# A three-layer kernel on one core: every step from the first load to the last store in one written list, in a new order

## The chip, the cores and the metric

The kernel runs on one core of one Trainium2 chip. The metric is the device time in microseconds (us) of that core, the median of several executions. One more execution was profiled, and all rows below come from it. Its engines are called PE (TensorE), DVE (VectorE), ACT (ScalarE), POOL (GpSimd) and SP (SyncE, whose queue issues the transfers).

## The reference

Three layers follow one another (float32 throughout):

```python
scores = scale * q @ k.T                    # 4 batches x 8 heads, 576 tokens, 64 wide
masks  = local (last 32 keys) for heads 0-3, strided (same position mod 32) for heads 4-7
attn   = softmax(where(mask, scores, -1e9)); x = (attn @ v) as 2304 x 512

h = relu(x @ w_in) ** 2                     # 512 -> 2048
x = h @ w_out                               # 2048 -> 512

logits = x @ phi                            # 2304 x 32 slots
d = softmax(logits, over the tokens); slot_input = d.T @ x
slot_out[e] = relu(slot_input[e] @ w1[e]) @ w2[e]     # 8 experts, 4 slots each
out = softmax(logits, over the slots) @ slot_out
```

## The kernel before, in words

The tokens go in five blocks of 512, 512, 512, 512 and 256. The hidden width of the second layer is cut into 16 pieces of 128, so that there are 80 **steps** (16 to a block, `NSTEP`). One step is 12 matmuls of 128 by 128 by 512 (by 256 in the last block), issued by `gemm1` in four quarters of three: a product of a high and a low part in a reduced float format. Its result lies in one of two PSUM buffers called `h`. `square` takes it out with a relu (token R), `sq` squares it (X; on ACT, or on POOL for some early steps), `bt_` turns it in 32x32 blocks on DVE (T), and `logits` multiplies four steps at a time with a folded matrix `pt` (L), in four column strips of the array.

At the end of each block `Dispatch` carries a running softmax over the tokens: `copy`, `total` (two full-array matmuls and a maximum), `turn`, `slots` (up to 64 small products in 32x32 tiles of the array, into the PSUM tile `four`), `sums` (adds them to the block sums) and `comb` (the softmax over the slots). The last block has its own path, `last_turn` and `last_sums`, after which the expert layer runs: `slot_in`, `sit`, `gemm_a`, `relu`, `turn`, `gemm_b`, `slot_out` and `output`. While the last step's softmax runs, `hold` issues five dummy matmuls.

Beside this run 16 attention units (`Unit`, token A: four masks and score products per batch, a softmax on DVE, ACT and POOL, turned weights, value products) and 24 conversions (`convert`, token C), which unpack weights that lie in memory as 64-bit words. Their PE work uses the array in strips of 32 or 64 columns, except masks and subtractions.

**What sets the order.** Each engine has its own queue and takes its instructions in the order in which the program issues them; only semaphores tie the queues together. Up to step 17 the order is a written list of tokens, `HEAD`, each a letter, a number and sometimes an engine (`A0P` is the next step of unit 0, on POOL). From step 18 on, a loop issues the four quarters of each step in turn, and after each quarter what a table of positions says (`AT`, `OFF`, `WO_AT`, `D_AT`, `LATE_T` and others):

```python
for kc in range(4):
    if s >= HEAD_STEPS:
        gemm1(s, (0, 2, 1, 3)[kc:kc + 1])
    if kc == 3 and s >= HEAD_STEPS:
        (last_step if s == NSTEP - 1 else square)(s)
    for fn, args in bg.get(4 * s + kc, ()):
        fn(*args)
```

The expert layer is plain straight code after the loop. The 64 weight tiles of the experts (512 KB each) are loaded in one fixed order `e_order` by `load_e`, each into a buffer that something else has left; SP issues them in program order and waits there for the buffer.

Of the kernel before, what the change touches and what calls it, by code (L numbers as in the profile page):

```python
# [29 lines left out]
OLD_AT = (8, 6)  # L30
# [3 lines left out]
WO_AT = [91, 117, 154, 170, 199, 219, 235, 249]  # L34
AT = [76, 89, 101, 115, 131, 150, 163]
OFF = [0, 7, 8, 12, 23]
# [3 lines left out]
w9 A0 A0 A0D A0P A0 A0 A0P A0A A2P q2 A2P A2 A0D w6 l2 C1 l3 C1 C1 A2P A2D A2 A2 A0P A0A A0A A0A A0A A0A A0A C1D q1  # L40
A1D A1P A1A A1 l1 v0 A0A A0A A2D C1 C1P C1P C1D A1A A1D A1 A2 A2D A2D A1 l0 C0 C0 A2A A2A A2A A2A A2A A2A C0 A1D C1P
C0 A3 A0A q3 A3 A3 A0 A0A A1A A3D C0 C0A C0P C0P A0A A0 A1A A1A A1D A3D A1A A3D v2 A2A A2D A3A A1A A1A A1A A1A G0 l5
l4 C2P C2P A3P A3P A2D A2D A2D A2 C0P A2 A3A A2 A2A v1 A1D G0 G1 A3A A3A A3A C2 A1 A1A A1P C2P C2 C2P A1 l6 q4 A4D A4
G1 C3D A3A A3A A3A A3A l7 C3 A4D A4D A4 v3 H A3A A3 C3 A3 C3P A3 C3 A3 C3 C3P C3P C2 A3 A3 A3 A3 G0 G1 G1 A4A R1 G0 R0
A5A C3D C2D A4D A4D l9 l10 C5D l11 C5 C5 C5 C5 l8 C4D C4 C4 C4P C4 C4D C4P C5 C5P C5D C5P G3 G3 G3 G3 R3 C2D G4 G4 G4
G4 q5 l17 A4 A5A A5 A5 l16 C8 C8 l12 C6 R4 C8 C4P C8 l14 l13 C6D C6 C6 G2 G2 A5 A5P A5 A5D A4P C4P G2 G2 C7 l18 A5D
X4A C6 R2 l15 C7 C7P l19 C9 C9D C9 C7 C9 C8 A4A C7D C9P A4A A5A C7P C6 A4A C7P C7P G5 A6 G5 G5 G5 G6 G6 G6 G6 G7 G7 G7
q6 A6A A6 l21 f P0 G7 A6D G9 G9 R5 A4D T4 X3D R6 P0 P0 A4A A4A R7 A5 C6D C6P X1D A4A Z v4 A4 A5P A6P A6P A5 X0A P0 C7P
X2A T1 T2 A4 A4A A5 A5 A4 A4A A4 C6P A4 G9 G9 G10 G10 G8 G8 G8 A5 l23 l20 C10P C10D C10D C10 R9 C10P l24 l22 C11 C11
C11 C11 C11 A4A A4P A6 X7A T7 A6P A6P A6A G10 G10 P1 P1 G8 v5 q7 A7 A7A G11 C12 R8 X6A A7P l25 C12 C12 G11 G11 G11 R10  # L50
C12 C12 X5A R11 A7D A7D A5 G14 A6P A6D l26 X9D A7A A7P A7D A7D A5 A7A A7P A7D A5 A7A A5P C13 l27 C13 C13 A7A A5A C13
C13 A5 G12 G12 G12 G12 R12 X12A T3 A7A A7P G14 G14 G14 R14 T0 G13 G13 P1 P1 P2 L0 P2 P2 P2 T9 l28 C14A q8 v6 A6A l29
C14 X14A A6A A6A A6 C14 X11A X8D A6P A7A A6 A6 G15 G13 G13 R13 C14 l30 C15 A8A L1 A6P A6 v7 A8 A8 C14P A8 A8A X13A
X10A T5 A7P A7A A7 A7 A7A A8P l31 C15 C15 A8 A8 C15 A8D T11 G15 G15 G15 T10 G17 G17 G17 G17 G16 G16 G16 G16 C15D P3
A8P A8D A8 A8 A8 R15 X15D A8 A8 A8 A8 L2 T15 P3 P3 P3 v8 A8 T8 A8 R16 A8D A8 A8 T13 T12 T6 T14 R17 L3
"""
FILL = 6
HEAD_STEPS = 18
AT_LAST = 40
ATT_END = 48  # L60
D0_AT = [1, 9, 11, 14, 17, 19]
D_AT = [3, 6, 7, 12, 13, 17]
DZ_AT = [7, 11, 17, 23, 30, 32]
LATE_T = 16
LATE_L = 22
LG_OFF = 19
LATE_TZ = 26
LATE_LZ = 37
EPS = 1e-9
HOLD = [5, 0, 0]  # L70
# [22 lines left out]
def body(tc, qd, kd, vl, vs, win, wout, woutt, phi, w1, w2, cst, out):  # L93
# [3 lines left out]
    with ExitStack() as base, ExitStack() as order:  # L97
# [464 lines left out]
        class Dispatch:  # L562
            def __init__(self, b):
                self.b, self.T = b, TB[b]
                self.n = TB[b] // 128
                self.cv = c_all[:, 4 * b:4 * b + self.n, :]

# [44 lines left out]
            def sums(self):  # L612
                for n in range(2):
                    to, flat = acc[:, 2 * DM * n:2 * DM * n + 2 * DM], four_[n].rearrange("p a z -> p (a z)")
                    if self.b >= KEEP:
                        return
                    if self.b:
                        DVE.scalar_tensor_tensor(out=flat if self.b == KEEP - 1 else to, in0=to, scalar=al, in1=flat, op0=ALU.mult, op1=ALU.add)
                    else:
                        DVE.tensor_copy(to, flat)  # L620

            def last_turn(self):
                z = [slice(0, 128), slice(128, 256)]
                e_ = gk_[0][:, 0:256]
                for n in range(2):
                    ACT.activation(e_[:, z[n]], self.o[:, z[n]], AF.Exp, bias=nm, accum_out=(bs, bs2)[n])
                    DVE.transpose(out=lsb[:, z[n]], in_=e_[:, z[n]])
                ACT.activation(al, nm_run, AF.Exp, scale=-1.0, bias=nm)
                DVE.tensor_scalar_mul(tal, tident[:, 0:NS], al)
                ov = self.o[:, 0:256].rearrange("p (c a i) -> p c a i", a=4, i=32)  # L630
                for a in range(4):
                    DVE.transpose(out=self.cv[q(a)], in_=ov[q(a), :, a, :])

            def last_sums(self):
                o = [ps("h", f"accT{x}") for x in range(2)]
                old = gk_[0][:, OLD:OLD + 2048].rearrange("p (a z) -> p a z", a=4)
                to = {}
                for x in range(2):
                    for n, copy in enumerate((ACT.copy, DVE.tensor_copy)):
                        z = 2 * x + n  # L640
                        to[x, n] = (lsb if z == 3 else gk_[0][:, 512 * z:512 * z + 512]).rearrange("p (a i) -> p a i", a=2)
                        copy(to[x, n], four_[n][:, :, 256 * x:256 * x + 256])
                for x in range(2):
                    for a in range(4):
                        PE.matmul(o[x][q(a), 0:256], tal, old[:, a, 256 * x:256 * x + 256], start=True, stop=False, skip_group_check=True)
                for x in range(2):
                    hold(HOLD[1 + x])
                    for a in range(4):
                        PE.matmul(o[x][q(a), 0:256], tident[:, 0:NS], to[x, a // 2][:, a % 2], start=False, stop=True, skip_group_check=True)
                    DVE.transpose(out=gT[:, 8 * x:8 * x + 8, :].rearrange("p f s -> p (f s)"), in_=o[x][:, 0:256])  # L650
# [86 lines left out]
        convs = [convert(m) for m in range(16)]  # L737
        mats = [matrix(h) for h in range(4)]
        gemms = {s: iter((0, 2, 1, 3)) for s in range(HEAD_STEPS)}
# [7 lines left out]
        for token in HEAD.split():  # L747
            k, e = token[0], token[-1] if token[-1] in ENG else ""
            n = int(token[1:].rstrip("ADP") or 0)
            if k == "f":  # L750
                SP.dma_start(ph, phi)
            elif k == "q":
                load_qk(units[n].b, units[n].p, units[n].u)
            elif k == "v":
                load_v(units[n].b, units[n].p, units[n].u)
            elif k == "l":
                load_w(n)
            elif k == "w":
                for _ in range(n):
                    PE.matmul(warm, dummy, dummy, start=True, stop=True)  # L760
            elif k == "A":
                units[n].step(e)
            elif k == "C":
                next(convs[n])(e)
            elif k == "P":
                next(mats[n])()
            elif k == "G":
                gemm1(n, (next(gemms[n]),))
            elif k == "R":
                square(n, e)  # L770
            elif k == "X":
                sq(n, e)
            elif k == "T":
                bt_(n)
            elif k == "L":
                logits(0, n)
            elif k == "H":
                headx.close()
                gp.append(pool(base, "gp", reuse_waits="tile"))
                gt_.append(gp[0].tile([128, SB * 512], F32, name="gt"))  # L780
                gk_.append(gp[0].tile([128, NG * 512], F32, name="gk"))
            else:
                psx.close()
                lgp = pool(lgx, "lgp", space=PSUM, reuse_waits="tile")
                four_.extend(lgp.tile([128, 2, 512], F32, name=f"four{n}") for n in range(2))

        bg = {}

        def at(p, fn, *args):
            bg.setdefault(p, []).append((fn, args))  # L790

        end0 = 4 * SB
        last = AT_LAST
        for n, p in zip(range(9, 4 + len(UNITS)), AT):
            un = units[n]
            at(max(end0, last + 3), load_qk, un.b, un.p, un.u)
            at(max(end0, last + OFF[4]), load_v, un.b, un.p, un.u)
            for k, o in zip("SCETV", OFF):
                at(p + o, un.run, k)
            last = p  # L800
        for b in range(NBLK):
            e = end0 * b
            late_t, late_l = (LATE_TZ, LATE_LZ) if b == NBLK - 1 else (LATE_T, LATE_L)
            if b:
                for f in range(SB):
                    p = 4 * (SB * b + f) + 4
                    at(p, sq, SB * b + f)
                    at(max(p, e + late_t), bt_, SB * b + f)
# [43 lines left out]
        for n in range(3):  # L852
            at(WO_AT[0] - 16 + n, load_wo, n)
# [244 lines left out]
```

## Time and profile before

| | us |
|---|---|
| median of 3 executions | 376.4 (376.33 to 376.76) |
| the profiled execution, its own time | 375.84 |
| its span, first to last instruction | 373.8 |
| PE busy in it | 361.2 |
| DVE / ACT / POOL busy | 243.8 / 173.5 / 63.8 |

The span is what the rows divide; 2.04 us of the profiled execution's own time lie around it. Busy time of PE is modelled from pipelined matmuls, so a busy PE can still lose time between two matmuls; the lengths of runs of matmuls in the chain show that better than the busy share.

### The profile page before, as it was taken

What the parts mean: (1) busy time and instruction counts of PE and PEld (TensorE: products, weight loads), DVE (VectorE), ACT (ScalarE), POOL (GpSimd) and SP (SyncE); (2) the same over time, 40 slices, a digit from 0 to 9 for tenths busy, and PEclk for the clock granted to TensorE, in tenths of its full rate; (3) what the DMA queues carried; (4) which work ended last, traced back from release to release, by engine and by line L of the source; (5) the groups of instructions that cost most, each with busy time, mean ns of one, the idle gap of its engine ahead of it and who ended that gap; (6) DMA issues with size and microseconds to landing.
All of it is one profiled execution on the core that took longest, in us unless ns stands there. A gap on an engine that the chain in (4) does not pass through costs nothing.

```text
span 373.8 us, 9705 instructions
## 1 busy us (share of the span) xinstructions
PE 361.2 (97%) x4062; PEld 260.4 (70%) x4062; DVE 243.8 (65%) x516; ACT 173.5 (46%) x373; POOL 63.8 (17%) x96
## 2 busy tenths in 40 slices
PE   8979999999999999999999999999999999999993
PEld 7767876676756687786677877667778698534783
DVE  2798999999997698787598763484243454432251
ACT  1697594555532454453246435425454445211241
POOL 7153339210120012020002100000000000262000
PEclk9999999999999999999999999999999999999999
DMA  8999966566516026334123158240318999999986
GB/s 233 359 350 351 393 212 225 167 211 185 187 45 246 3 67 210 94 121 119 60 63 107 50 196 302 91 183 15 115 56 289 413 408 357 335 400 412 407 346 240
DMA packets 25356, 80.59 MB, mean 216 GB/s; under 512 B 3041, under 2 KB 3297, under 8 KB 25313
## 3 DMA queue, kind: packets, MB, share of 16 engines
q1 hardware_dynamic: 25072, 79.53, 59.7%
q8 instruction: 32, 0.52, 0.6%
q10 hardware_dynamic: 240, 0.44, 0.5%
q14 instruction: 12, 0.09, 0.1%
HBM read 75.25 MB, written 4.72 MB: 214 GB/s over the span
## 4 chain that ended last, share of the span: by engine, by line
PE 80%; DVE 13%; issue 2%; POOL 2%; ACT 2%; DVEq 0%; ACTq 0%; POOLq 0%
PE h L479 47%; PE four L608 6%; PE so L983 4%; PE eh L956 4%; PE oa L396 3%; PE four L532 2%; PE lg L532 2%; DVE y L454 2%; DVE ptl L366 1%; PE out L1001 1%; DVE wo L454 1%; PE ob L396 1%; PE qa L291 1%; DVE w L463 1%; DVE tiny L322 1%
## 5 line engine op out<-in xcount | busy, mean ns | idle before, releaser
L479 PE MATMUL h<-x,w 128*128 128x512 f32 x768 | 188.3, 398 | 0.2 <-ACT gk L498 0.2
L479 PEld LDWEIGHTS h<-x,w 128*128 128x128 f32 x768 | 140.9, 188 | 46.1 <-issue 15.2
L498 ACT ACTIVATE gk<-h 128x512 f32<-128x512 f32 (+1 forms) x70 | 38.4, 551 | 86.5 <-PE h L479 86.2
L511 DVE STREAM_TRANSPOSE gt<-gk 128x512 f32<-128x512 f32 (+1 forms) x71 | 44.3, 640 | 44.7 <-ACT gk L502 39.0
L502 ACT ACTIVATE gk<-gk 128x512 f32<-128x512 f32 (+1 forms) x68 | 39.5, 584 | 1.4
L479 PEld LDWEIGHTS h<-xl,w 128*128 128x128 f32 x192 | 23.6, 191 | 3.5 <-issue 3.4
L479 PE MATMUL h<-xl,w 128*128 128x256 f32 x192 | 25.0, 287 | 0.0
L366 DVE STREAM_TRANSPOSE ptl<-sl 32x320 f32<-32x320 f32 (+1 forms) x48 | 23.7, 493 | 0.7
L447 ACT ACTIVATE wo<-raw 128x512 f32<-128x512 f32 x32 | 20.8, 669 | 5.8 <-DVE w L463 3.7
L454 DVE SCALAR_TENSOR_TENSOR wo<-raw,wo 128x512 uint32<-128x512 uint32 x32 | 22.3, 715 | 0.2
L608 PE MATMUL four<-gt,lsb 32*32 32x512 f32 x576 | 21.3, 598 | 0.0
L608 PEld LDWEIGHTS four<-gt,lsb 32*32 32x32 f32 x576 | 9.7, 103 | 8.5 <-issue 3.8
L412 DVE TENSOR_TENSOR x<-oa,x 128x512 fp32r<-128x512 f32 (+1 forms) x16 | 10.7, 666 | 6.9 <-ACT x L411 4.6
L463 POOL TENSOR_TENSOR w<-y,w 128x512 fp32r<-128x512 f32 x11 | 15.0, 1373 | 0.6 <-ACT w L459 0.5
L817 POOL COPY lsb<-pt 128x128 f32<-128x128 f32 x1 | 0.3, 289 | 84.8 <-PE four L608 84.8
L983 PE MATMUL so<-e,gk 128*32 128x128 f32 (+1 forms) x304 | 14.7, 302 | 0.0
L956 PE MATMUL eh<-e,lsb 128*32 128x512 f32 x104 | 14.3, 594 | 0.4 <-DVE lsb L934 0.4
L366 DVE STREAM_TRANSPOSE pts<-sw 32x512 f32<-32x512 f32 x20 | 14.0, 700 | 0.7 <-POOL sw L331 0.5
L459 POOL CAST w<-y 128x512 fp32r<-128x512 f32 x9 | 8.8, 985 | 30.9 <-DVE y L454 7.6
L411 ACT CAST x<-oa 128x512 fp32r<-128x512 f32 (+1 forms) x15 | 9.0, 601 | 10.8 <-PE oa L396 10.5
L315 POOL TENSOR_TENSOR sl<-sl,tiny 128x640 f32<-128x640 f32 x4 | 5.4, 1340 | 49.4 <-DVE tiny L314 49.4
L450 DVE TENSOR_SCALAR wo<-wo 128x1024 uint32<-128x1024 uint32 x16 | 12.5, 784 | 0.7 <-ACT wo L447 0.5
(231 smaller groups left out, 480.8 us busy)
## 6 DMA issues: line engine op xcount, KB each, us to landing
e<-w SPq DMA_DIRECT2D x50, 512.0 KB, 8.1
raw<-win SPq DMA_DIRECT2D x16, 512.0 KB, 8.2
raw<-woutt SPq DMA_DIRECT2D x16, 512.0 KB, 4.9
raw<-wout SPq DMA_DIRECT2D x16, 512.0 KB, 4.0
q<-qd SPq DMA_DIRECT2D x16, 288.0 KB, 4.4
out<-ob SPq DMA_DIRECT2D x12, 384.0 KB, 4.2
k<-kd SPq DMA_DIRECT2D x29, 144.0 KB, 4.2
v<-vs SPq DMA_DIRECT2D x8, 512.0 KB, 4.9
```

The source lines that it names most:

```text
L366: yield "T", lambda e, d=dst, s_=src: DVE.transpose(out=d, in_=s_)
L396: PE.matmul(o[bank][d0, col:col + w1_ - w0], u.v[0:k, t, d0], rhs, start=start, stop=stop, skip_group_check=True)
L447: ACT.activation(y[0][:, z], raws[2 * m + z][:, :, 1].bitcast(F32), AF.Prelu, scale=2.0 ** -112, alpha=2.0 ** 32)
L454: DVE.scalar_tensor_tensor(out=yb, in0=raws[2 * m + z][:, :, 0], scalar=29, in1=yb, op0=ALU.logical_shift_right, op1=ALU.bitwise_or)
L463: ENG[e].tensor_tensor(out=w[:, 1], in0=y[0][:, z], in1=w[:, 0].bitcast(F32), op=ALU.subtract)
L479: PE.matmul(hs[s][0][:, 0:TB[b]], w_in[s % SB][:, a, 128 * kc:128 * kc + 128], x_of(b, kc)[:, x, :] if b < 4 else xl[:, :, kc, x, :], star ...
L498: ACT.activation(gs[s], h[:, 0:TB[s // SB]], AF.Relu)
L502: ACT.activation(gs[s], gs[s], AF.Square)
L511: DVE.transpose(out=by_tokens(b)[:, :, f, :] if b else gt_[0].rearrange("p (f t) -> p f t", f=SB)[:, f], in_=gs[s])
L608: PE.matmul(four_[a // 2][q(c % 4), a % 2, :], ext[q(a), c, :], g[q(a), c] if self.b else g[q(a), :, 32 * c:32 * c + 32], start=c < 4 and ...
L956: PE.matmul(hps[g][n][q(j), :], siT[:, kc, :], cols(et[0, g, j, kc], 512 * n, 512), start=kc == 0, stop=kc == 3, skip_group_check=True)
L983: PE.matmul(sums[n][q(j)], hT[g][fc // 4][:, fc % 4, q(j)], cols(et[1 + n, g, j, wd * fc // 1024], wd * fc % 1024, wd), start=g == 0 and f ...
```

## The change

`HEAD` now holds all tokens from the first load to the last store, with new letters for the later work (D for the parts of `Dispatch`, K for one dummy matmul, E `gemm_a`, z a part of `gemm_b`, F one output product and its copy, d one output store, and lower-case letters for expert loads). The loop, its tables and the straight code go. The functions keep what they compute; `last_turn`, `last_sums`, `turn`, `output` and others are cut into pieces so that each piece can stand anywhere. PE gets the same matmuls as before, five dummies among them. What differs, besides the order:

- the first block's sums are copied by ACT (one half) and DVE, before by DVE alone;
- 21 of the 79 relus of `square` are on DVE, before none;
- 31 of 79 squares are on POOL, before 5 (a token `X..D` takes the POOL branch of `sq`);
- 21 of the copies of attention values out of PSUM are on DVE, before 5;
- in the last six output products DVE copies the first, third and fifth result, before ACT did;
- the steps of the second layer are no longer in rising order.

```diff
-OLD_AT = (8, 6)
-WO_AT = [91, 117, 154, 170, 199, 219, 235, 249]
-AT = [76, 89, 101, 115, 131, 150, 163]
-OFF = [0, 7, 8, 12, 23]
...
-HEAD_STEPS = 18
...
-D_AT = [3, 6, 7, 12, 13, 17]
...
-HOLD = [5, 0, 0]
...
 HEAD = """
...
+q2 w9 A2P A0 A0 A0D A0P A0 A0 A0P A0A A0P A2P w6 A1D l2 C1 l3 C1 A2 A2P A2D C1 A0P A0A A0A A0A A2 A0A C1D C1 A0A A0A
+q1 A1P A1A C1P C1P A2 A2P A1 C1D A0A A0A A1A A1D A1 A3 l0 C0 l1 C0 A2 A2D A2A A1 A2A A2A v0 A0A A2A A2A A2A A2A C0 A0
...
+D0 T8 D0 G20 G20 G20 G20 G19 G19 G19 G19 T14 R18 T13 R20D l32 q9 v9 A9P D0 A9P T17 T16 R19 A9P A9P A9P X18A C16 A9P
...
+G59 G59 G63 G63 G63 C23 C23 C23 C23 R59 X62D G60 G60 G60 G60 R60D G63 T57 X59A X58D L14 X60A T60 G64 G64 G64 R63 X63D
...
+G68 G68 G71 G71 G71 G71 G69 G69 G69 G69 G70 D3 D3 R68 R71 R69 x1 x2 i0 c0 c1 i1 s0 r0 r1 r2 s1 s2 s3 s4 G70 G70 G70
...
+X64A T64 D3 G77 G77 R77D G75 G75 G75 G75 R75 T65 D3 X73D X75D X77A T67 G76 G76 G76 G76 G78 G78 G78 G78 G79 R76 X76D m0
+T70 L16 L17 L18 T71 T73 T77 T75 T74 R78 X78A T76 T72 o1 T78 L19 D4 o0 G79 G79 G79 R79 T79 K0 D4 u3 T66 a0 K0 K0 K0 K0
+a1 V0 D4 b1 b3 B0 b0 N0 b2 Q0 B1 N1 u0 s5 g0 s6 s7 s8 s9 s10 s11 I0 I1 I2 s12 s13 s14 s15 i2 g1 s16 s17 s18 s19 x3 x4
+I3 x5 x6 p0 S0 E1 E0 E2 W0 M3 u1 p1 S1 E3 k0 k1 k2 k3 c0 E4 E5 c1 r0 r1 r2 E9 E8 E10 E6 E12 E7 k4 k5 s0 s1 s2 u2 D4 U0
...
+z5 z5 z5 z5 z5 z5 z5 F16 F17 d8 F15A F14D d7 z5 z5 z5 z5 z5 z5 z5 z5 t2 F18D F19A d9 F20D F21A d10 F22D F23A d11
 """
...
-                        DVE.tensor_copy(to, flat)
-
-            def last_turn(self):
...
+                        (DVE.tensor_copy if n else ACT.copy)(to, flat)
+
+            def last_exp(self, n):
                 e_ = gk_[0][:, 0:256]
...
+            def last_scale(self):
                 ACT.activation(al, nm_run, AF.Exp, scale=-1.0, bias=nm)
                 DVE.tensor_scalar_mul(tal, tident[:, 0:NS], al)
...
+            def last_copy(self, z):
+                x, n = divmod(z, 2)
+                t = self.to[x, n] = (lsb if z == 3 else gk_[0][:, 512 * z:512 * z + 512]).rearrange("p (a i) -> p a i", a=2)
+                (DVE.tensor_copy if n else ACT.copy)(t, four_[n][:, :, 256 * x:256 * x + 256])
...
+        def hold(n):
+            PE.matmul(late_ps("at", "hold0")[:, 0:256], ident, c[:, 0:256], start=True, stop=True)
...
+        def product(x, e):
+            d, n, z = x // 6, x // 2 % 3, x % 2
+            o = late_ps(("h", "at", "h", "at", "t")[x % 5], f"out{d}{n}{z}")
+            PE.matmul(o[:, 0:TO], tiles["s4"][:, 1, 128 * d:128 * d + 128],
+                      cT[n][:, 3 * z:3 * z + 3, :].rearrange("p a b -> p (a b)"), start=True, stop=True)
+            (DVE.tensor_copy if (e or "AD"[x % 2]) == "D" else ACT.copy)(ob(d, n)[:, z], o[:, 0:TO])
...
+        for token in HEAD.split():
...
+            elif k == "R" and n == NSTEP - 1:
+                last_step(n)
+            elif k == "R":
+                square(n, e)
...
+            elif k == "D":
+                next(disps[n])()
```

## Rows read from the trace of the kernel before

**Rows 1.** The page: busy time and share of the span of each engine, and instructions.
```profile
PE 361.2 (97%) x4062; PEld 260.4 (70%) x4062; DVE 243.8 (65%) x516; ACT 173.5 (46%) x373; POOL 63.8 (17%) x96
```

**Rows 2.** Stretches: length, busy PE, PEld, DVE, ACT, POOL (instructions), granted clock, DMA share, GB/s.
```profile
0.00:30.00 30.00, 25.52 (x382) 21.11 (x383) 19.52 (x50) 17.70 (x43) 13.74 (x28) 1.00 0.97 320
30.00:120.00 90.00, 88.48 (x934) 63.34 (x948) 83.81 (x161) 50.81 (x107) 26.93 (x23) 1.00 0.65 222
120.00:160.00 40.00, 40.00 (x460) 29.29 (x435) 31.83 (x67) 17.79 (x35) 5.95 (x6) 1.00 0.30 94
```

**Rows 3.** Waits of TensorE: who was waited for, us, times, longest.
```profile
PE wide L271 <- DVE tiny L265: 1.3, 2, 0.7
```

**Rows 4.** The chain that ended last, 240 to 300 us: start, length, what.
```profile
252.15 9.07 PE h L479 x39
261.22 1.00 PE lg L532 x8
262.21 11.11 PE h L479 x48
...
288.21 0.86 PE lr L576 x2
```

**Rows 5.** Groups by line and shape, VectorE: busy, mean ns, idle before.
```profile
L463 DVE TENSOR_TENSOR w<-y,w 128x512 fp32r<-128x512 f32 x5 | 4.6, 950 | 0.0
...
L620 DVE COPY acc<-four 128x1024 f32<-128x1024 f32 x2 | 2.3, 1194 | 0.0
...
L459 DVE CAST w<-y 128x512 fp32r<-128x512 f32 x2 | 1.6, 808 | 0.0
...
L642 DVE COPY gk<-four 128x512 f32<-128x512 f32 x1 | 0.7, 691 | 1.8 <-PE four L608 1.8
...
L411 DVE CAST x<-oa 128x256 fp32r<-128x256 f32 x1 | 0.6, 610 | 0.0
...
L411 DVE CAST xl<-ob 128x64 fp32r<-128x64 f32 x1 | 0.2, 224 | 0.0
```

**Rows 6.** Line 504, the squares on GpSimd: ns least/median/most, first and last start.
```profile
L504 POOL TENSOR_TENSOR gk<-gk x2: 1042/1266/1490, 74.2 to 103.6; 128x512 f32<-128x512 f32 x2
```

**Rows 7.** Line 450 on VectorE, same columns.
```profile
L450 DVE TENSOR_SCALAR wo<-wo x16: 650/684/1657, 47.3 to 279.2; 128x1024 uint32<-128x1024 uint32 x16
```

**Rows 8.** Order of time, 45 to 52 us: start, length, engine, line.
```profile
45.52 4.55 POOL L463 TENSOR_TENSOR w<-y,w 128x512 fp32r<-128x512 f32 x3
...
47.26 1.66 DVE L450 TENSOR_SCALAR wo<-wo 128x1024 uint32<-128x1024 uint32 x1 [0.49 <-ACT wo L447]
```

**Rows 9.** Order of time, 312 to 332 us.
```profile
317.03 0.67 PE L578 MATMUL lr<-gk,lsb 128*128 128x256 f32 x2 [0.27 <-ACT gk L520]
...
317.54 2.32 PE L895 MATMUL hold<-c 128*128 128x256 f32 x10
...
319.79 2.38 PE L608 MATMUL four<-gt,lsb 32*32 32x512 f32 x64
...
328.63 1.92 PE L956 MATMUL eh<-e,lsb 128*32 128x512 f32 x16 [0.37 <-DVE lsb L934]
```

**Rows 10.** Order of time, the last 20 us.
```profile
363.23 3.29 PE L983 MATMUL so<-e,gk 128*32 128x128 f32 x64
...
367.74 1.24 ACT L1003 COPY ob<-out 128x384 f32<-128x384 f32 x3 [0.91 <-PE out L1001]
367.91 1.49 DVE L1003 COPY ob<-out 128x384 f32<-128x384 f32 x3 [0.71 <-PE out L1001]
```

**Rows 11.** SyncE queue: loads of the last layer, first two and last groups.
```profile
220.20 9.20 SPq L683 DMA_DIRECT2D e<-w  x7
...
247.69 0.86 SPq L683 DMA_DIRECT2D acc<-w  x2
...
340.90 9.26 SPq L683 DMA_DIRECT2D e<-w  x8
```

**Rows 12.** The page, transfers: issues, KB each, median us from issue to landing.
```profile
e<-w SPq DMA_DIRECT2D x50, 512.0 KB, 8.1
```

More of the change, by code (lines that the diff above doesn't have):

```diff
@@ L787, in body @@
[L787 to L808, printed above, removed]
-                for ch in range(4 if b < NBLK - 1 else 3):
-                    at(max(e + 16 * ch + LG_OFF, e + late_l), logits, b, ch)
-            if b < NBLK - 1:
-                d = Dispatch(b)
-                for o, f in zip(D0_AT if b == 0 else DZ_AT if b == NBLK - 2 else D_AT, (d.copy, d.total, d.turn, d.slots, d.sums, d.comb)):
-                    at(e + end0 + o, f)
@@ L824, in body, with tile_of, late_ps, bt @@
-        cs4, cT, co = {}, {}, {}
-        def weights(n, eng):
+        gT = pt
+        siT = lsb[:, 0:128].rearrange("p (a b) -> p a b", a=4)
+        rsum = st[:, 14:15]
+        tiles = {}
+        def tile_of(name, make):
+            if name not in tiles:
+                tiles[name] = make()
+            return tiles[name]
+        def late_ps(tag, name):
+            return tile_of(name, lambda: ps(tag, name))
+        def bt(n):
+            return gk_[0][:, 512 * n:512 * n + 512]
+        def hT(g, n):
+            return bt(2 + 2 * g + n).rearrange("p (a b) -> p a b", a=4)
@@ new lines, in relu, with turn @@
+        def relu(x):
+            g, n = divmod(x, 2)
+            if n:
+                DVE.tensor_scalar(bt(1), hps(g, 1), rsum, 0.0, op0=ALU.mult, op1=ALU.max)
+            else:
+                ACT.activation(bt(0), hps(g, 0), AF.Relu, scale=rsum)
+        def turn(x):
+            g, n = divmod(x, 2)
+            ht = late_ps("mo" if n else "t", f"ht{g}{n}")
+            for z in range(4):
+                h_ = bt(n)[:, 256 * (z // 2):256 * (z // 2) + 256].rearrange("p (x a) -> p a x", a=2)[:, z % 2, :]
+                PE.matmul(ht[:, 128 * z:128 * z + 128], h_, ident, start=True, stop=True, is_transpose=True)
@@ L846, in weights_t, with weights_out @@
                           is_transpose=True)
[L848 removed]
+        def weights_out(x, e):
+            n, z = divmod(x, 2)
             cT[n] = cs4[n]
[L850 to L860 removed]
@@ L862, in body, with sums @@
-        for s in range(SB, NSTEP + 1):
-            if s == ATT_END:
+            (DVE.tensor_copy if (e or "DA"[z]) == "D" else ACT.copy)(cT[n][:, 3 * z:3 * z + 3, :].rearrange("p a b -> p (a b)"),
+                                                                      tiles[f"ct{n}{z}"][:, 0:384])
+        cuts = [slice(0, 256), slice(256, 384), slice(384, 512)]
+        def sums(n):
+            o = late_ps(("t", "lg", "t")[n], ("so0", "so1", "so0")[n])
+            return o[:, (0, 0, 256)[n]:(256, 128, 384)[n]]
@@ new lines, in output, with load_e_one, final @@
+        def output(x):
+            d, n = divmod(x, 3)
+            t0 = 2 * TO * n
+            SP.dma_start(out[128 * d:128 * d + 128, t0:t0 + 2 * TO], ob(d, n).rearrange("p a b -> p (a b)"))
+        def load_e_one(x):
+            load_e(lambda name: ring(x // 4, x % 4, [128, 2, 512], F32, name))
+        def final(n):
+            lgx.close()
+            late.append(pool(base, "late", space=PSUM, reuse_waits="tile"))
+        parts = [parts_b(n, g) for n in range(3) for g in range(2)]
+        plain = {"K": hold, "u": lambda n: d.last_turn(n), "a": lambda n: d.last_exp(n), "V": lambda n: d.last_scale(),
+                 "b": lambda n: d.last_copy(n), "B": lambda n: d.last_old(n), "N": lambda n: d.last_new(n), "Q": final,
+                 "I": slot_in, "p": si_copy, "S": sit, "M": lambda n: POOL.memset(bt(2 + n), 0.0), "E": gemm_a, "U": inverse,
+                 "W": weights, "J": relu, "h": turn, "O": weights_t, "z": lambda n: next(parts[n]), "t": slot_out, "d": output,
+                 "k": load_e_one}
```

444 lines of the change are left out of this document (166 added, 278 removed).

## The prediction

> **What bounds the kernel now.** I read the page's busy times first, then the stretches, TensorE's waits, the chain that ended last, and the order of time where the chain leaves TensorE. The page says that TensorE is busy 361.2 of 373.8 us [rows 1], so at most 12.6 us are idle. The stretches show where: 4.48 us lie in the first 30 us, and from 30 to 160 us TensorE lacks only 1.52 us [rows 2]. TensorE's list of waits is short: its longest total is 1.3 us, for a maximum in the first units [rows 3]. So neither idle time nor waits hold much, and the matmuls themselves do not change.
>
> What is left is time that TensorE loses while it counts as busy. The chain gives it. A run of 39 matmuls of the second layer takes 9.07 us and one of 48 takes 11.11 us [rows 4]. The nine more cost 2.04 us, 0.2267 us each. But 48 times that is 10.88 us, so each run pays 0.23 us once for having been interrupted. The interruption between them is a product with the folded matrix in four column strips: 8 records, two passes for each of 4 strips side by side, 1.00 us [rows 4]. Two such passes over 512 columns on the whole array, the `total` of a block, take 0.86 us [rows 4]. So the strips lose another 0.14 us, and one **visit** from the full array to strips or small tiles and back costs 0.14 + 0.23 = 0.37 us without any idle time.
>
> The second resource is VectorE. From 30 to 120 us it is busy 83.81 of 90 us, from 120 to 160 us 31.83 of 40 [rows 2], so it nearly ties with TensorE there. It has 6.19 + 8.17 = 14.36 us to spare until 160 us.
>
> **The change part by part.**
>
> *Fewer visits.* I wrote both orders down as TensorE's queue sees them and counted the visits (a `total` or a dummy uses the full array and makes none). Until 64 quarter steps have been issued, both orders make 16. After that the order of before makes 29 until the last step, the new one 16: attention products, `slots` and L products now stand side by side, as L16, L17 and L18 do. 13 visits by 0.37 us are 4.8 us. Inside a merged visit the array may still go from strips to 32x32 tiles; such inner changes rise from 6 to 11 in all. No row prices one by itself: five more cost between nothing and half a visit each, 5 by 0.185 = 0.9 us. I take half, 0.5, since strips to tiles is the same kind of change in small: **-4.3 us** (-4.8 to -3.9).
>
> *The end of the last block.* One dummy now stands before `total`. Before, TensorE idled 0.27 us there for the last square, with a further gap inside the busy time, and the five dummies (10 records, 2.32 us) ended at 319.86, where `slots` began at 319.79 [rows 9]. With four after the maximum, `slots` may come up to 0.4 us earlier: -0.4. The first product of the expert layer waited 0.37 us for a VectorE turn [rows 9]; now the second copy stands behind that turn: -0.2. Against this, VectorE has seven turns, a copy of 1024 columns and another turn (about 5 us by the order) just before the last step's square, in some 4.5 us of TensorE work: +0.2 (nothing to +0.5). The output products stood in four groups and stand in five, one visit more: +0.3. At the very end VectorE's three copies take 1.49 us and ScalarE's 1.24, and VectorE began 0.17 us later [rows 10]; starting it first saves that: -0.2. Together **-0.3 us** (-1 to +0.6).
>
> *The head.* The two masks that were issued late are now issued ahead of products, into the holes of the first 30 us. 15 dummies, the loads and their order stay. Of 4.48 idle us [rows 2] and the 1.3 us wait [rows 3], I take **-0.5 us**; the bounds are -2 (half of the idle time closes) and +1.5 (a mask in front of something that was ready).
>
> *Work moved to VectorE and GpSimd.* Up to step 27 the new order puts 8 relus on VectorE. No row has a relu there; the nearest is its copy of 128x512 out of PSUM, 0.691 us [rows 5]: 5.5 us. 7 more copies of attention values come, some of 0.61, some of 0.22 us [rows 5]: 2.8 us. Two weight subtractions more (0.95 each) and two casts fewer (0.81 each) give +0.3, and half of the first block's sums goes, 1.19 us [rows 5]. That is 7.4 us more on VectorE in the stretch where 14.36 are free. The free time is partly waiting that new work cannot fill, so I let a part show: **+0.7 us** (nothing to +7.4). ScalarE has room for its half of the sums: it idles more than half of the span [rows 1]. If that cover went, it would cost one copy of 1024 columns, 1.19 us by VectorE's row.
>
> *GpSimd's squares.* 31 squares go there, before 5. One takes between 1.04 and 1.49 us [rows 6]. Each is off TensorE's path as long as the turn behind it isn't due. What they can do to VectorE the trace shows once: while GpSimd ran three subtractions on end from 45.52 on, VectorE's shift at 47.26 took 1.66 us [rows 8], where the median of that line is 0.684 [rows 7]. So an overlap can cost VectorE 1.0 us. Up to step 27 the new order has 8 squares on GpSimd where 5 were, three more, so at most +3 us where VectorE is tight; the other 23 fall later, and after 160 us VectorE has 243.8 - 135.2 = 108.6 us of work in 213.8 [rows 1, 2]. I take nothing for it in the sum and keep +3 for the range. The Trainium skill (GPSIMD Engine Reference, Specifications) says that GpSimd's SBUF interfaces are shared with VectorE and contend with instructions with two SBUF inputs or in a two-port mode; the shift row agrees with it. By that rule, at the row's price, the three squares would make the sum below 3.0 us larger, 375.0 for a median; without it the sum stands as it is.
>
> *Order of the expert loads.* Only the first stands early in the list (x0), eight others that were issued at 220 and 247 us [rows 11] stand behind step 69. But SP's queue runs ahead of the others: between x0 and those eight there is nothing else on it, so they start when x0 does and their buffers are free. That is after the last conversion of weights, in the new order near step 57, some 260 us. The fixed order of the tiles stays. I count nothing.
>
> **Sum.** -4.3 - 0.3 - 0.5 + 0.7 = -4.4 us against the profiled execution's own 375.84: 371.4. The median of the runs shown is 376.4, 0.56 above that execution, so for a median I forecast 371.4 + 0.6 = **372.0 us**.
>
> **The rivals.**
>
> *The head closes too.* Half of the 4.48 idle us and the whole visit price: 376.4 - 4.8 - 0.3 - 2.2 = **369.1**. For it: only that stretch has idle time on TensorE. Against it: 15 dummies and the first loads stay.
>
> *VectorE becomes the bound, slower.* It gets 7.4 us by step 27 and up to 3 from GpSimd, 10.4 in all, and of its 14.36 idle us it can fill only a share. The other terms give -5.1. With half of it filled, 10.4 - 7.2 = 3.2, and the kernel still gains; with a quarter, 10.4 - 3.6 = 6.8 and it ends 1.7 us slower, **378.1**. It decides from where less than 10.4 - 5.1 = 5.3 of the 14.36 us are of use. For it: 83.81 of 90 us busy. Against it: turns and subtractions may lie behind TensorE for some microseconds, since their results are due only at the end of a block.
>
> *The changes of shape stay.* If a merged visit pays inside what it saves outside (an L product behind `slots` drains the array all the same), the first term is near nothing and head, end and VectorE cancel: **376.3**. Against it: inner changes rise by only 5, and the two passes of `total` show that the price belongs to the shape.
>
> *Loads late, slower.* If the nine early tiles only start after 280 us, nine of 512 KB at the spacing of the last group (9.26 us for 8 [rows 11]), 10.4 us, come onto a queue that is full until 350 us. The last eight tiles, issued until 350.16 [rows 11], land 8.1 us later [rows 12], at 358.3, and the last 64 products, which use half of them, start at 363.23 [rows 10], so 5.0 us of delay are free: 376.4 - 4.4 + 5.4 = **377.4**. It needs the last conversions to be late by 20 us.
>
> **How the numbers follow.** Forecast 0.60 (its own range 370 to 374.6), head closes 0.17, shapes stay 0.08, VectorE 0.11, loads 0.04. The range 368.3 to 376.6 holds the forecast, most of the head case and the shapes case, some 0.83; it leaves out the two slower cases. 0.2% of 376.4 is 0.75 us, about what a measurement of this kernel can tell from no change. Faster by more: 0.60 + 0.17 and a little of the rest, 0.78. Within: 0.08. Slower: 0.11 + 0.04, less what ends even, 0.14.
>
> **What would show it.** In the profile of the changed kernel: TensorE's busy time about 4 us lower, its runs of second-layer matmuls longer and fewer, 0.2267 us each as before. From 30 to 160 us VectorE busy some 7 us more, TensorE still without idle time there. `slots` of the last block right behind the fourth dummy. It is wrong if TensorE's waits name a VectorE relu or a turn, if idle time appears between 100 and 170 us, if VectorE's two-input instructions lengthen in the stretches with GpSimd's squares, or if weight loads in the last 40 us wait for a transfer.

## The result, and the profile after

The changed kernel takes 373.24 us in the median of 4 runs (372.71 to 373.84), the kernel before 376.49 (4 runs, 376.33 to 376.76). The ratio is 0.9913, with a 95% interval of 0.9896 to 0.9931: 3.25 us faster, where 4.4 were forecast. The profiled execution took 373.05 us, its span 371.2.

The page's busy times and the stretches, with the columns of [rows 1] and [rows 2]:

```profile
PE 357.3 (96%) x4062; PEld 262.1 (71%) x4062; DVE 260.0 (70%) x557; ACT 144.0 (39%) x308; POOL 82.6 (22%) x120
...
0.00:30.00 30.00, 24.48 (x383) 20.05 (x384) 19.09 (x50) 17.28 (x40) 16.99 (x31) 1.00 0.97 312
30.00:120.00 90.00, 88.58 (x883) 64.72 (x897) 83.44 (x165) 47.93 (x100) 23.93 (x22) 1.00 0.63 212
120.00:160.00 40.00, 39.40 (x575) 29.22 (x544) 34.18 (x74) 13.63 (x26) 8.46 (x9) 1.00 0.38 117
```

TensorE is busy 3.9 us less, as foreseen. But against [rows 2] it has 0.60 us of idle time from 120 to 160 us, which the prediction had named as a sign that it was wrong, and VectorE is busy only 2.0 us more from 30 to 160 us (83.44 + 34.18 against 83.81 + 31.83), not 7.

The price of an interruption is unchanged. This is the chain that ended last around 270 us, start, us, what (compare [rows 4]):

```profile
267.76 0.99 PE lg L548 x8
268.76 11.11 PE h L495 x48
279.87 0.99 PE lg L548 x8
280.87 3.82 PE h L495 x30
```

What is new stands in the merged visits. The chain again, at 144 and at 224 us, each from the end of one run of second-layer matmuls to the start of the next:

```profile
144.00 0.69 PE qa L324 x53
144.68 0.88 PE four L548 x7
145.56 0.35 issue
145.91 1.24 PE oa L412 x32
147.16 0.18 PE ob L412 x16
147.34 2.76 PE h L495 x11
...
224.52 0.99 PE four L548 x8
225.52 0.50 PE oa L412 x32
226.02 0.50 PE ob L412 x32
226.52 1.83 PE four L548 x8
228.35 2.97 PE h L495 x12
```

At 145.56 TensorE stands for 0.35 us. The value products read attention weights that VectorE turns (L382), and the last of these turns ends at 145.82; the first weight load of the products starts at 145.88. In VectorE's queue the turns stand behind subtractions for the values of the unit before (L428). The timelines (columns: start, us, engine, line, operation, operands, idle time before):

```profile
144.63 0.22 DVE L428 TENSOR_TENSOR xl<-ob,xl 128x32 fp32r<-128x32 f32 x1
144.86 0.96 DVE L382 STREAM_TRANSPOSE ptl<-sl 32x320 f32<-32x320 f32 x2
145.88 1.00 PEld L412 LDWEIGHTS oa<-ptl,v 128*32 128x32 f32 x32 [1.23 <-issue]
```

A third merged visit, at 155.7 us, has 0.25 us of idle time at 157.84, for another reason. There the value products need a PSUM buffer that the scores just before still hold, and the reading of the scores (L314), which ends at 157.99, stands behind a relu that now lies on VectorE (L512). The two waits make the 0.60 us of idle time above:

```profile
156.51 0.69 DVE L512 TENSOR_SCALAR gk<-h 128x512 f32<-128x512 f32 x1
157.23 0.76 DVE L314 SCALAR_TENSOR_TENSOR sl<-qa,c 128x128 f32<-128x128 f32 x2
158.06 0.56 PEld L412 LDWEIGHTS oa<-pts,v 128*32 128x32 f32 x32 [1.13 <-issue]
```

The visit at 224 us shows no idle matmul at all, but its second L product takes 1.83 us where one alone takes 0.99. The weight loads and GpSimd's timeline give the reason:

```profile
227.30 0.14 PEld L548 LDWEIGHTS four<-gk,pt 128*32 128x32 f32 x2 [0.84 <-POOL gk L520]
...
226.21 1.04 POOL L520 TENSOR_TENSOR gk<-gk 128x512 f32<-128x512 f32 x1 [6.13 <-ACT gk L514]
```

The product waits 0.84 us for the square of step 47, which GpSimd ends only at 227.25.

The end of the last block, TensorE's timeline (before: [rows 9, 10]):

```profile
314.18 0.67 PE L595 MATMUL lr<-gk,lsb 128*128 128x256 f32 x2
314.68 1.89 PE L786 MATMUL hold<-c 128*128 128x256 f32 x8
316.53 2.37 PE L625 MATMUL four<-gt,lsb 32*32 32x512 f32 x64
...
325.44 1.07 PE L821 MATMUL eh<-e,lsb 128*32 128x512 f32 x8 [0.37 <-DVE lsb L807]
...
364.76 1.53 PE L906 MATMUL out<-c,s 128*128 128x384 f32 x6 [0.75 <-DVE s L897]
```

By milestones, after less before: first matmul of step 18 109.56 against 110.69, -1.1 us, with the same matmuls behind it; last `total` 314.18 against 317.03, -2.85; `slots` 316.53 against 319.79, -3.26; first expert product -3.19; last output products 364.76 against 367.26, -2.50; end of the span -2.6. So in this pair of executions **the head gave 1.1 us, the middle 1.7, and the end of the last block with the expert layer gave back 0.25**.

The middle, from step 18 to the last `total`, can be added up from TensorE's rows. The second layer has 744 matmuls there in both kernels: before they stand in 33 runs of 156.25 us together, after in 20 runs of 153.65 us, so 13 fewer runs save 2.6 us. The 28 visits before take 47.18 us, and the 15 of the changed kernel, 13 fewer, take 47.91: the visits themselves gave nothing.

One execution is not the kernel. In e7 and e12 below, whose lists are the same in the middle, it takes 203.98 and 203.96 us, in this execution 204.62 and before 206.34. So the middle gained 1.7 us in this execution and 2.4 us in those two. The difference lies in one visit, shown under e3.

### The profile page after: what moved, and what is told of

The parts are those of the page before. It is cut to its first block, busy times and chain, and to the rows that moved or that the text cites. A ratio compares the mean times of both kernels' runs of the same rounds, so it can differ in the third digit from the quotient of the medians.

```text
span 371.2 us, 9694 instructions
## 1 busy us (share of the span) xinstructions
PE 357.3 (96%) x4062; PEld 262.1 (71%) x4062; DVE 260.0 (70%) x557; ACT 144.0 (39%) x308; POOL 82.6 (22%) x120
## 3 DMA queue, kind: packets, MB, share of 16 engines
HBM read 75.25 MB, written 4.72 MB: 215 GB/s over the span
## 4 chain that ended last, share of the span: by engine, by line
PE 71%; DMA 12%; DVE 10%; POOL 2%; ACT 2%; issue 1%; SPq 0%; POOLq 0%; ACTq 0%
PE h L495 41%; PE four L625 6%; DMA raw<-win 5%; PE so L889 4%; PE eh L821 4%; DMA raw<-woutt 3%; PE four L548 2%; PE oa L412 2%; DVE ptl L382 2%; DMA k<-kd 2%; PE lg L548 2%; DMA v<-vs 2%; PE out L906 1%; DVE wo L470 1%; DMA q<-qd 1%
## 5 line engine op out<-in xcount | busy, mean ns | idle before, releaser
L495 PE MATMUL h<-x,w 128*128 128x512 f32 x768 | 184.9, 397 | 0.0
L514 ACT ACTIVATE gk<-h 128x512 f32<-128x512 f32 (+1 forms) x51 | 28.3, 555 | 81.3 <-PE h L495 63.6
L520 POOL TENSOR_TENSOR gk<-gk 128x512 f32<-128x512 f32 (+1 forms) x29 | 27.4, 954 | 103.4 <-ACT gk L514 83.8
L527 DVE STREAM_TRANSPOSE gt<-gk 128x512 f32<-128x512 f32 (+1 forms) x71 | 42.9, 629 | 9.7 <-PE four L625 6.0
L518 ACT ACTIVATE gk<-gk 128x512 f32<-128x512 f32 (+1 forms) x41 | 23.5, 591 | 8.4 <-DVE gk L512 8.1
L382 DVE STREAM_TRANSPOSE ptl<-sl 32x320 f32<-32x320 f32 (+1 forms) x48 | 23.7, 494 | 3.7 <-POOL sl L347 2.9
L512 DVE TENSOR_SCALAR gk<-h 128x512 f32<-128x512 f32 (+1 forms) x19 | 11.6, 610 | 18.1 <-PE h L495 16.2
L466 DVE TENSOR_SCALAR wo<-wo 128x1024 uint32<-128x1024 uint32 x16 | 11.0, 686 | 10.9 <-ACT wo L463 10.6
L382 DVE STREAM_TRANSPOSE pts<-sw 32x512 f32<-32x512 f32 x20 | 14.0, 702 | 1.4 <-POOL sw L347 1.1
L475 POOL CAST w<-y 128x512 fp32r<-128x512 f32 x10 | 7.4, 746 | 28.8 <-ACT gt L514 11.7
L889 PEld LDWEIGHTS so<-e,gk 128*32 128x32 f32 x304 | 11.5, 110 | 3.2 <-issue 1.3
L548 PE MATMUL four<-gk,pt 128*32 128x512 f32 x78 | 11.9, 596 | 0.0
```

The lines of the kernel that those rows point to most:

```text
L382: yield "T", lambda e, d=dst, s_=src: DVE.transpose(out=d, in_=s_)
L495: PE.matmul(hs[s][0][:, 0:TB[b]], w_in[s % SB][:, a, 128 * kc:128 * kc + 128], x_of(b, kc)[:, x, :] if b < 4 else xl[:, :, kc, x, :], star ...
L514: ACT.activation(gs[s], h[:, 0:TB[s // SB]], AF.Relu)
L518: ACT.activation(gs[s], gs[s], AF.Square)
L520: POOL.tensor_tensor(out=gs[s], in0=gs[s], in1=gs[s], op=ALU.mult)
L527: DVE.transpose(out=by_tokens(b)[:, :, f, :] if b else gt_[0].rearrange("p (f t) -> p f t", f=SB)[:, f], in_=gs[s])
```

## The experiments

All medians are of repeated runs beside the kernel before on the same chip. It took 376.3 us (17 runs) beside e1 to e4, 376.63 (14 runs) beside e5 to e8 and 376.66 (13 runs) beside e9 to e12. The changed kernel was not run again beside them, and its 373.24 us stood beside 376.49: a difference from it of less than some 0.4 us decides nothing.

| run | us, median (range) | ratio to before | 95% interval |
|---|---|---|---|
| e1 relus on ScalarE | 380.04 (379.91 to 381.82) | 1.0095 | 1.0062 to 1.0129 |
| e2 squares on ScalarE | 383.96 (383.09 to 386.70) | 1.0196 | 1.0157 to 1.0234 |
| e3 four visits apart | 372.59 (372.33 to 372.61) | 0.9885 | 0.9852 to 0.9918 |
| e4 `slots` in four groups | 377.60 (376.84 to 379.65) | 1.0032 | 1.0010 to 1.0053 |
| e5 before, relus on VectorE | 380.33 (379.29 to 381.55) | 1.0093 | 1.0061 to 1.0125 |
| e6 before, squares on GpSimd | 379.39 (378.82 to 380.90) | 1.0067 | 1.0040 to 1.0093 |
| e7 four output groups | 372.96 (372.36 to 374.12) | 0.9901 | 0.9871 to 0.9932 |
| e8 apart, later, four groups | 373.80 (373.37 to 374.43) | 0.9918 | 0.9889 to 0.9947 |
| e9 before, both moves | 383.71 (383.06 to 384.99) | 1.0196 | 1.0176 to 1.0216 |
| e10 new order, no moves | 388.94 (387.36 to 391.43) | 1.0341 | 1.0312 to 1.0371 |
| e11 apart, weights later | 372.46 (371.86 to 373.04) | 0.9893 | 0.9878 to 0.9908 |
| e12 old head | 374.40 (373.91 to 375.33) | 0.9947 | 0.9933 to 0.9962 |

**e4, the price of a visit.** `slots` of blocks 0 to 3 is issued in four parts, a quarter of the second layer between them:

```
-for c in range(num):
+for c in range(num) if part is None else range(4 * part, 4 * part + 4):
...
-... D2 T49 T51 X50D L12 T50 G57 G57 G57 R57 X57A D2
+... D2 G57 D2 G57 D2 G57 D2 T49 T51 X50D L12 T50 R57 X57A D2
```

> The price of a visit by itself: the changed kernel with the slot products of blocks 0 to 3 in four groups of 16 matmuls each, a quarter of the first product between the groups, instead of one run of 64. The same matmuls on the same engines, 12 more visits. If a visit costs 0.37 us, as lone visits do in the trace of before, 12 times 0.37 is 4.4 us later than the changed kernel, that is 377.6. If a visit is worth what the 13 fewer of the change brought by the traces (2.0 us, 0.15 each), 1.8 us later, 375.0. If nothing is paid for a visit, no change.

Measured 377.60, which is 4.36 us above the changed kernel, 0.36 us for each of the 12 visits. That is the number expected, but the trace shows that it agrees by luck. TensorE has a wait for a relu there that the changed kernel does not have:

```profile
206.50 4.39 PE L496 MATMUL h<-x,w 128*128 128x512 f32 x18 [1.90 <-ACT gk L515]
```

`slots` of block 1 ends later in this list, VectorE starts to add it to the block sums at 191.48 us instead of 188.55, and what stands behind that on VectorE and ScalarE is later too; which step of it delays the relu was not tested. What a visit itself costs stands in the chain, in the runs behind it:

```profile
121.97 1.07 PE four L626 x32
123.05 0.90 PE h L496 x3
123.95 1.07 PE four L626 x32
125.02 0.90 PE h L496 x3
```

Three matmuls take 0.90 us where 3 times 0.2267 are 0.68: 0.22 us for the run. But four parts of `slots` take 4 x 1.07 = 4.28 us, and `slots` in one piece takes 4.42 in the chain of the changed kernel (293.64 us), so that a part costs nothing by itself. Summed over the middle, 12 more runs take 4.72 us more than in e7 and e12, 1.9 of it the wait, and the visits 0.4 us less. A visit more therefore costs about 0.2 us here. The 0.23 us in the run behind a visit stands; the 0.14 us that the prediction found for strips does not hold for the tiles of `slots`. For strips it agrees with another row: value products straight behind an L product take 0.50 us for their first part (225.52 in the chain above), alone 0.64 (224.00 in the chain of before). What is missing in the middle is therefore to be looked for inside the merged visits.

**e3, four merged visits apart.** Only TensorE's order changes, and what hangs on it; the second of four such edits, and the last:

```
-L6 v11 A11P T24 ... C18 G28 G28 G28 G28
+L6 v11 G28 G28 A11P T24 ... C18 G28 G28
-X47D L11 A15D D2 A15D A15P T45 A15P G48 G48 G48 ... D2 R48 G51 G51
+X47D A15D A15D A15P T45 A15P G48 G48 L11 D2 G48 ... R48 G51 D2 G51
```

> The changed kernel with four merged visits pulled apart again by quarters of the first matrix product: the values of units 10 and 11 behind 3 and 2 quarters instead of straight behind the scores and the logits; one quarter before and one behind the slot products of block 1; the last logits of block 2 two quarters later. Five more visits than the changed kernel. Theory A (each of these four holds a wait of 0.25 to 1 us for VectorE or GpSimd, 2.3 us in all, and a lone visit costs 0.37): the four lost 4.1 us as they are, nine lone ones 3.3, so 0.8 us earlier (0.2 to 1.5). Theory B (no wait is at stake, only the number of visits): five visits more at 0.15 to 0.37 each, 0.75 to 1.85 us later.

Measured 372.59, 0.65 us below the changed kernel with five visits more (0.46 if each is compared with the kernel before beside it), and no run as slow as its fastest. The chain at the places of the visits at 144 and 224 us:

```profile
144.65 0.69 PE qa L324 x54
145.33 0.88 PE four L548 x7
146.21 2.29 PE h L495 x9
148.50 1.17 PE oa L412 x32
149.67 0.17 PE ob L412 x16
149.84 2.26 PE h L495 x9
...
224.59 0.99 PE four L548 x8
225.58 0.50 PE oa L412 x32
226.08 0.50 PE ob L412 x32
226.58 1.59 PE h L495 x6
228.17 0.99 PE four L548 x8
229.17 2.30 PE h L495 x9
```

The first visit took 3.34 us merged (144.00 to 147.34) and takes 1.56 + 1.34 = 2.90 in two; the second 3.83 merged and 1.99 + 1.00 = 2.99 in two. The other two, from the same view, took 3.54 and 7.66 and take 3.21 and 6.95. Together the same products cost 18.37 us merged and 16.05 apart, 2.3 us less. But the last of the four did not wait because it was merged. In e7 it stands merged as well; these are the slot products inside it, in the changed kernel and in e7:

```profile
183.44 5.10 PE four L625 x124
183.17 4.39 PE four L625 x121
```

With 4.39 the merged visit takes 6.95 us, as much as its three parts; so it does in e12. The 0.71 us more in the changed kernel's profiled execution are pauses between weight loads for which the profile names no cause; two other executions of the same orders there do not have them, so they belong to that execution and not to the list. So **three of these four visits take 1.6 us longer merged than apart**, and the waits shown above make 0.35 + 0.25 + 0.84 = 1.44 of it. Five more runs of second-layer matmuls pay 5 x 0.23 = 1.15 of that again, and 0.5 us are left: the middle takes 203.46 us here, 203.97 in e7 and e12. Theory A holds in its range, with waits in three visits and not in four; theory B falls. Theory B of e1, a price smaller than was taken, is right for the visits of `slots` (e4), and the waits stand beside it.

The engine alone does not make the wait at 224 us. In e2 below that square is on ScalarE, behind two casts, and the same visit takes 3.79 us; its L product stands as close behind the step that it needs:

```profile
233.40 0.14 PEld L548 LDWEIGHTS four<-gk,pt 128*32 128x32 f32 x2 [0.80 <-ACT gk L518]
```

**e1, e2, e10, e5, e6, e9: the moves in both orders.** In the list of the changed kernel the letter behind a relu (R) or a square (X) is taken away or turned, for 21 relus, for 31 squares, or for both:

```
-R30D R27 X30D ... T58 R67D X67D D3 D3
+R27 R30 X30D ... T58 R67 X67D D3 D3        (e1)
+R30D R27 X30A ... T58 R67D X67A D3 D3      (e2)
```

In the kernel before, `square` and `sq` ask for the step instead:

```
-if e == "D":
+if s in MOVED:      # the same 21 steps (e5, e9); in sq the same 31 (e6, e9)
```

> The changed kernel with all 21 moved relus back on ScalarE (one of them, of step 30, also one place later in ScalarE's list so that no buffer is waited for in a circle). Theory A (the visits that were put together now wait inside for VectorE): VectorE has 12.8 us less to do (21 times 0.61), the scores' buffers come free earlier, and the kernel ends 0.3 to 1.0 us earlier than the changed one, with the 0.60 us that TensorE lost between 120 and 160 us partly back. Theory B (the time lost is in the price of a visit, which is just smaller than was taken): nothing moves, within 0.3 us of the changed kernel. Theory C (ScalarE needed the relief): relus come late behind the copies of the values, the matmuls of the next step wait for the accumulator, 0.5 to 2 us slower.

> The changed kernel with the squares that GpSimd computes (31 in the list) on ScalarE, in the same places. Theory A: the visit with the values of the 16th unit and the last logits of block 2 no longer waits for step 47's square (TensorE's weight load waited 0.84 us for GpSimd there): 0.5 to 0.9 us earlier than the changed kernel if nothing else gets late. Theory B: within 0.3 us of it. Theory C (ScalarE needed the relief): 31 squares of 0.55 us make 17 us more on ScalarE, relus behind them come late, 0.5 to 2 us slower.

> The changed kernel's order without the two moves: all relus and all 31 squares on ScalarE (the relu of step 30 one place later in ScalarE's list). With one move undone it was 6.8 and 10.7 us slower than the changed kernel. Theory A (the new order lives off the moves): at least as slow as with one undone, 384 to 391. Theory B (the two belong together, order or not): back at 373 to 377, as a list that gives ScalarE its old work in one piece.

> The kernel before, in its own order, with the same 21 relus on VectorE as in the changed kernel. Theory A (in the old order no relu was late: TensorE waited 0.2 us for one in all; so the move is a cost, small while VectorE has room): 376.4 to 377.1, the 0.7 us that the prediction took. Theory B (VectorE becomes the bound, as the third rival of the prediction has it): 1.5 to 7.4 us slower than before. Theory C (the relus by themselves are what the change gains, whatever the order): 0.5 to 2 us faster than before.

> The kernel before, in its own order, with the 31 squares on GpSimd that the changed kernel has there (5 of another choice before). Theory A (nothing, as the prediction took: each square is wanted much later): 376.0 to 376.8. Theory B (squares of 0.95 to 1.1 us in place of 0.58 come late for the turns and the logits in an order that was not made for them, or slow VectorE down beside them): 0.8 to 3 us slower than before. Theory C (ScalarE's relief is worth something by itself): 0.5 to 1 us faster.

> The kernel before in its own order with both moves together: the 21 relus on VectorE and the 31 squares on GpSimd. By themselves the relus cost 3.7 us there and the squares 2.8. Theory A (each move puts an instruction behind something it did not stand behind in the old lists, and the new order was written round the moves): the costs stay, 3 to 6.5 us slower than before. Theory B (the two belong together: a relu early on VectorE makes up for a square late on GpSimd, in whatever order): within 1 us of before.

In the old order the relus cost 3.7 us, the squares 2.8 and both 7.1. In the new order it is the other way round: without the relus' move the kernel is 6.8 us slower, without the squares' 10.7, without both 15.7. The old list is not quite the reverse case: 5 squares, of its own choice, were on GpSimd there to begin with. Theory B for e5 and e6 holds, and theory A for e10. Theory A for e9 holds too, but 7.1 lies above its 3 to 6.5 us. For e1 and e2 only the direction of theory C is right: it allowed 0.5 to 2 us, and the loss is more than three and five times as large. The theory under which we ran e1 and e2, that the moves were what the merged visits wait for and would be better undone, fell.

Where it is lost can be named in two places. In e1 TensorE's waits have a new line, and ScalarE's timeline shows it at the `total` of block 3:

```profile
PE h L495 <- ACT gk L514: 2.8, 5, 1.1
PE lr L593 <- ACT lsb L586: 1.0, 1, 1.0
...
291.93 0.38 ACT L514 ACTIVATE gk<-h 128x256 f32<-128x256 f32 x1 [2.29 <-PE h L495]
292.21 0.58 ACT L586 COPY lsb<-lg 128x512 f32<-128x512 f32 x1
```

The list has step 67's relu ahead of the copy that `total` needs. On ScalarE the copy stands behind a relu that waits for its matmuls, and TensorE waits 1.00 us. In the changed kernel that relu is on VectorE, and the copy starts at 285.78, 0.1 us after the L product in front of it. In e9, the old order with both moves, the two largest waits that the kernel before did not have are of the same kind:

```profile
PE h L481 <- DVE gk L498: 2.0, 2, 1.1
...
PE four L534 <- POOL gk L506: 1.3, 1, 1.3
```

Two relus and one square there stand behind other work on their new engines. e5 and e6 have the same waits one by one, 2.0 us for the relus and 1.3 for the square.

**e12, the head.** The list up to the product of step 17 (520 entries) is that of the kernel before, the rest the new one.

> The changed kernel with its list up to the product of step 17 replaced by the list of the kernel before (its first 520 entries, with their engines), and behind it the rest of the new list in the new order. If the head is worth what the traces show at equal work (0.95 us), 374.2; if what the prediction took (0.5 us), 373.7; if the head gains nothing that lasts, 373.2.

Measured 374.40, 1.16 us above the changed kernel, and 0.99 if each is compared with the kernel before beside it. The new head is worth 1.0 to 1.2 us. A single trace cannot tell that: the first matmul of step 18 starts at 111.76 in this one and at 110.69 in that of the kernel before, with the same list up to there, and in e7 and e11, both with the new head, at 109.29 and 110.87.

**e7, e8, e11: the expert layer, and a better list.** e7 issues the output products in four groups of six:

```
-t0 F7 F4 F6 d3 F5 d2 F1 z3 ... t1 z4 z4 F0D F2 F11 F3A d1 d0 z4 z4 z4 z4 F9A ...
+t0 F7 F4 F6 d3 F5 d2 F1 F0 d0 z3 ... t1 z4 z4 F2 F3 d1 F8 F9 d4 F10 F11 d5 z4 ...
```

> The changed kernel with the output products in four groups of six, as before, instead of five. The prediction put the fifth group at 0.3 us; the traces show the expert layer 0.69 us longer than before. If the group is the cause: 0.3 to 0.7 us earlier than the changed kernel (372.5 to 372.9). If the expert layer lost it elsewhere: within 0.15 us of the changed kernel, or later, since six products in one group wait for the copies out of five accumulators.

Measured 372.96. The median is 0.28 us lower, but the trace speaks against the cause: from the first expert product to the last output products it needs 364.17 - 324.47 = 39.70 us, the changed kernel 364.76 - 325.44 = 39.32, the kernel before 367.26 - 328.63 = 38.63 [rows 9, 10]. e8, with the same four groups, needs 39.70 us again. The fifth group is not what the expert layer lost.

e8 adds e7's groups to e3, and issues unit 12's values two quarters later (`A13P G37 G37 A12P` for `A13P A12P`).

> The four visits pulled apart as in the run that did that (372.59), the values of unit 12 two quarters later as well (in that run's trace this visit still lost 0.78 us, a lone one that waits for nothing 0.3), and the output products in four groups. If the waits inside the visits and the fifth group are what the change gave back, 0.65 and 0.45 and 0.3 to 0.7 us earlier than the changed kernel: 371.4 to 371.9. If one of the two is not a cause, 372.2 to 372.6.

A miss: 373.80, slower than e3. The visit that was meant to gain lost the same as in e3, so it had not waited there, and the four groups cost 0.4 us as in e7; but everything behind unit 12 came later, and one relu with it, which TensorE now waits for:

```profile
PE h L495 <- ACT gk L514: 0.9, 1, 0.9
```

e11 adds to e3 that the transposes of the second pair of combine weights (`O3`, and `y3D` behind it) stand behind the first sums.

> The four visits pulled apart (372.59 by themselves), and in the expert layer the second pair of transposes of the combine weights after the first sums instead of before them: in the changed kernel's trace these three transposes and the next group stand 0.3 us longer among the expert products than in the kernel before, which did not have them there. If they wait there for GpSimd's weights: 0.3 us less than the visits apart alone, 372.1 to 372.4, and 0.3 us less between the first expert product and the last output product. If not: 372.5 to 372.9.

Measured 372.46, 0.1 us below e3. From the first expert product (325.58) to the last output products (364.83) it needs 39.25 us, 0.07 less than the changed kernel: the three transposes cost nearly the same in their new place. So what made the expert layer 0.69 us longer stays open; the number of groups and the place of these transposes are not it. Of all lists, e3 and e11 are the fastest; their medians lie 0.65 and 0.78 us under the changed kernel and their intervals overlap with its interval. The gain of e3, some 0.5 us, rests on its trace above all.

## Why the prediction was right

The forecast was 372.0 us, the measured time 373.24; it lies in the likeliest case and in its own range. The mechanism, fewer visits of TensorE away from the full array, was right. The sizes were off, and partly against each other:

- *Fewer visits, -4.3: the mis-sized term.* The count was right: the traces have 13 fewer visits and 13 fewer runs. So was the part of the price that is paid in the run behind a visit, 0.23 us, and 13 fewer runs saved 2.6 us. The other part, 13 x 0.14 = 1.8 us less in the visits themselves, did not come: 15 visits take 47.9 us (47.3 in e7 and e12) where 28 took 47.2. For the visits of `slots` there was nothing of it to save (e4). In place of the rest e3 shows 1.6 us lost inside three merged visits, most of it waiting for VectorE's turn of attention weights, for its reading of the scores and for a square of GpSimd. The prediction priced inside a merged visit only the inner changes of shape, +0.5. It did not ask what a merged visit puts next to what: value products straight behind the turn of their weights, scores and value products that share buffers, and an L product straight behind the square it reads. Measured, the term is about -2.5 (by e7 and e12).
- *Work moved, +0.7.* This term stood for free time of VectorE that new work cannot fill. In the new order the moves save time (e1, e2, e10), and of a cost the traces show one wait of 0.25 us behind a moved relu, at 157.84. That the +0.7 covers part of the waiting in the merged visits is luck: the two terms make -3.6, and the middle gained 2.4 us (1.7 in the profiled execution). Of GpSimd's squares the prediction said that they lie off TensorE's path as long as the turn behind them isn't due; here it was an L product that waited. The bound that it worked out for VectorE alone, 7.4 us, is close to what both moves do in the old order (7.1 us, e9), but by their places in the queues, not by a full engine: in e9 TensorE's largest new waits are two for relus and one for a square.
- *The signs.* Two of those that the prediction named for being wrong did appear, idle time of TensorE between 100 and 170 us and, in the timeline though not in the list of waits, a wait for a turn of VectorE. They pointed at what the merged visits lost.
- *The rival that VectorE becomes the bound* did not happen in the new order. e5 shows its direction where the order does not fit.
- *The rival that the changes of shape stay* is out as a whole: fewer runs did save 2.6 us. Half of it came true, since the merged visits ate what they were to save inside; the rows show waits for that, and no drain was measured by itself.
- *Head, -0.5:* -1.0 to -1.2 by e12. Under-sized, within its bounds.
- *End of the last block, -0.3:* +0.25. `slots` came 0.41 us earlier, as forecast (0.4). The wait of 0.37 us ahead of the first expert product remained, so the 0.2 of that part did not come. From there to the last output products it is 0.69 us more, not 0.3; the reason given, a fifth group, is refuted by e7.
- *GpSimd's squares, nothing taken for contention:* right. VectorE's two-input shift-and-or on the output weights takes 736 ns in the mean in the changed kernel, 715 before, and 730 in e2 without those squares. The Trainium skill (GPSIMD Engine Reference, Specifications) lets one expect contention with such two-input instructions; with 31 squares in place of 5 these rows show 21 ns on each of 32, of which only 6 go with the squares in e2.
- *Expert loads, nothing:* no run here tested it, and no wait of TensorE in the last 40 us names a transfer.

With the middle of e7 and e12 the parts make -2.4 - 1.1 + 0.25, about the 3.25 us that were measured.

## What to carry to other kernels

A price per interruption, read from the chain, carries over for the part that was read: here 0.22 to 0.23 us in the run behind each one. What a merged interruption waits for inside shows only in part as idle time, so compare the length of each with the lengths of its parts issued alone, and do so in more than one execution: 0.7 of the 2.3 us found here belonged to a single one. A run that hits the expected number still has to be taken apart; 1.9 of e4's 4.36 us were a new wait. Where a result is computed (which engine) cannot be priced apart from the order: much the same 52 moves cost 7.1 us in one list and saved 15.7 in the other, because each in-order queue passes its waits on to whatever stands behind. When products are put side by side, ask for each what it reads, and leave a few matmuls between it and the engine that makes that.

## What was not expected of the hardware

That TensorE's busy time can hide a wait: a product of eight matmuls counted as busy for 1.83 us in place of 0.99 while its weight load waited 0.84 us for GpSimd. The Trainium skill (TensorEngine Tiling (Array Packing), Key Properties) says that changing the tiling mode drains TensorE. The traces agree with that: in e4's rows each run of full-array matmuls behind such a change is 0.22 us longer than its matmuls.
